# Whole chunks in each step, odd heads on the other partition half, and a fixed order to the end, in a delta-rule attention with an FFN behind it

## Chip, cores, metric

One core of a Trainium2 chip. The metric is device microseconds of a whole execution, median of the runs named. Engines: PE is TensorE, DVE VectorE, ACT ScalarE, POOL GpSimd, SP SyncE.

## The reference

```python
# attention: batch 4, heads 8, sequence 768, head_dim 48
k_n = k / (np.linalg.norm(k, axis=-1, keepdims=True) + 1e-06)
for t in range(S):
    y[:, :, t] = einsum('bhd,bhde->bhe', q[:, :, t], state)
    v_old = einsum('bhde,bhd->bhe', state, kt)
    state = state + bt * einsum('bhd,bhe->bhde', kt, vt - v_old)
# FFN: 3072 tokens, d_model 384 (= 8 heads * 48), d_ff 1536
g = x @ w_gate
out = (g / (1 + exp(-g)) * (x @ w_val)) @ w_out
```

The weights are float64 and are converted to float32 on the core; q, k, v and beta are float32. Both kernels take the sequence in 12 chunks of 64 steps. Inside a chunk the recurrence becomes matrix products: the Gram matrix K K^T is masked (call it M), the inverse Z^T of a triangular matrix made of M and beta is computed, then with the state S of the chunk before: r = V - K S, u = Z r, S += K^T u, y = Q S + (masked Q K^T) u. y of a chunk is the input x of its FFN. A 64x64 inverse is made of two 32x32 halves, done on DVE for 128 (head, half) pairs at once (`invert`), and a corner block by small matmuls (`join`).

## The kernel before: what the change touches

A unit of work is two batches of one chunk (`n`); a chunk has two units, and a group of two chunks is inverted at once.

```python
ORDER = ((0, 0), (1, 1), (0, 1), (1, 0))          # (par, b): head parity, batch
def advance(n, ps):                                # one unit
    ...                                            # K S and Q S of a unit into one p_y, r = V - K S
    yield
    for j in range(NP):
        for par, b in ORDER:
            rows = slice(64 * b, 64 * b + 64)
            nc.tensor.matmul(p_u[rows, par, j], zt[rows, u, 2*j+par], r[rows, par, j], ...)
    nc.scalar.copy(uu, p_u)
    yield
    ...                                            # S += K^T u (rows of b to rows of par)
            nc.tensor.matmul(ys[rows, par, j], pq[rows, 2*j+par], uu[rows, par, j], ...)
    nc.scalar.copy(heads(y), ys)
    yield
    ...                                            # three transposes of y, copy to x_ffn

with tc.manual_schedule(engines={PE, ACT, DVE, SP}):
    ...                                            # start, chunk 0's FFN with the weights' conversion
nc.gpsimd.memset(ztp[1], 0.0)                      # from here the compiler's scheduler orders
some(invert(1), everything)
some(joins(1, ps_one), everything)
for c in range(1, NCH):
    ...
    for bp in range(NB):
        some(advance((c + 1) * NB + bp, ps_one), everything)
    feed = ffn(c)
    for n in range(FT // 2 + NB):
        some(feed, 3 if n < FT // 2 else 1)
        some(behind, 2)                            # preparation of a later group
```

A matmul reads its two operands from the partitions of one half and writes the half in which its output lies. In p_u and in the second part of p_y, rows `b` go to rows `b`: two of the four 64x64 tiles of the array.

## Time and profile before

| | us |
|---|---|
| median of 3 runs | 907.58 (907.29 to 911.88) |
| the profiled run: metric, span | 904.54, 902.7 |
| FFN of chunk 1 starts at | 190.1 |
| from there to the last matmul | 708.4, of it PE idle 32.9 (7.9 for kn, 6.2 for the state, 6.0 for r, 9.3 around the joins and masks, 2.1 for h_f) |
| changes between 128x128 and smaller tiles in that stretch | 216 (counted record by record; the prediction has 217) |

A row of a timeline gives start, length, engine, line, operation, output<-inputs, shape and count, and in brackets the idle time before it and what ended it. The rows overlap at their ends, since ends of pipelined matmuls are modelled; differences of starts are the safe reading. In the trace each fp32 matmul of the program is two records (32 matmuls of `p_s` are "x64" for a whole chunk), transposes are one. The prediction below shows the lines.

### The profile page before, as it was taken

How to read it: one execution, taken by the hardware profiler on the slowest of the kernel's cores; microseconds unless marked ns; L12 is line 12 of the kernel's file. 1: busy time of each engine (PE TensorE's matmuls, PEld its weight loads, DVE VectorE, ACT ScalarE, POOL GpSimd, SP SyncE). 2: the span in 40 equal slices, each digit the busy share in tenths (PEclk: the TensorE clock that was granted, in tenths of full speed). 3: DMA queues.
4: the chain of work that ended last, by engine and by line, in shares of the span. 5: the costliest groups of instructions: out<-in, count | busy, mean ns of one | idle time of the engine just before them, and what ended most of it. 6: DMA issues, size and time to landing. Idle time of an engine off the chain costs nothing.

```text
span 902.7 us, 19256 instructions
## 1 busy us (share of the span) xinstructions
PE 784.2 (87%) x8648; PEld 604.9 (67%) x8648; DVE 435.9 (48%) x883; ACT 153.0 (17%) x284; POOL 87.3 (10%) x100
## 2 busy tenths in 40 slices
PE   1407787698978999998999998999998999999998
PEld 1307575376757857867857867867867768778684
DVE  4799877997238912218912219913219812001010
ACT  1104323201212112111112111112111112011010
POOL 4000112100140002210002210003110000000000
PEclk9857889798999999999999999999999999999999
DMA  6324543410031000211010211010001000000000
GB/s 167 81 39 125 146 133 102 118 27 1 12 70 37 1 20 19 45 34 31 0 22 18 45 37 27 1 28 11 10 19 20 0 20 2 1 19 1 18 1 18
DMA packets 85171, 34.38 MB, mean 38 GB/s; under 512 B 78176, under 2 KB 81248, under 8 KB 85088
## 3 DMA queue, kind: packets, MB, share of 16 engines
q1 hardware_dynamic: 78240, 27.93, 13.2%
q10 hardware_dynamic: 6848, 5.21, 2.7%
q8 instruction: 68, 1.11, 0.5%
q14 instruction: 15, 0.12, 0.0%
HBM read 28.41 MB, written 4.72 MB: 37 GB/s over the span
## 4 chain that ended last, share of the span: by engine, by line
PE 57%; DVE 32%; issue 3%; POOL 3%; ACT 2%; ACTq 2%; DMA 1%; DVEq 0%
PE p_o L560 18%; PE p_gate L540 13%; PE p_val L540 12%; DVE zb L392 7%; DVE tmp L386 6%; DVE mb L357 3%; PE p_g L313 3%; POOL norm L284 2%; DVE zt L357 2%; PE p_u L476 2%; PE p_t L302 2%; DVE h_f L553 2%; PE p_j L428 1%; PE p_y L510 1%; DVE mb L355 1%
## 5 line engine op out<-in xcount | busy, mean ns | idle before, releaser
L540 PE MATMUL p_gate<-x_ffn,wg_sb 128*128 128x256 f32 x864 | 216.8, 394 | 9.5 <-DVE wg_sb L223 8.7
L540 PE MATMUL p_val<-x_ffn,wv_sb 128*128 128x256 f32 x864 | 208.9, 386 | 0.0
L560 PE MATMUL p_o<-wo_sb,h_f 128*128 128x384 f32 x576 | 199.9, 500 | 9.4 <-DVE wo_sb L223 7.3
L540 PEld LDWEIGHTS p_gate<-x_ffn,wg_sb 128*128 128x128 f32 x864 | 162.4, 194 | 34.1 <-DVE wg_sb L223 9.5
L540 PEld LDWEIGHTS p_val<-x_ffn,wv_sb 128*128 128x128 f32 x864 | 161.8, 191 | 23.1 <-issue 0.7
L560 PEld LDWEIGHTS p_o<-wo_sb,h_f 128*128 128x128 f32 x576 | 108.8, 194 | 84.0 <-DVE wo_sb L223 11.0
L553 DVE TENSOR_TENSOR h_f<-sil,p_val 128x512 f32<-128x512 f32 x72 | 49.2, 683 | 136.0 <-PE p_val L540 135.8
L549 ACT ACTIVATE sil<-p_gate 128x512 f32<-128x512 f32 x72 | 43.0, 597 | 221.8 <-PE p_gate L540 219.5
L386 DVE TENSOR_TENSOR tmp<-zb,mb 128x31 f32<-128x31 f32 (+15 forms) x186 | 63.6, 342 | 6.0
L392 DVE TENSOR_TENSOR zb<-zb,tmp 128x31 f32<-128x31 f32 (+15 forms) x186 | 63.6, 342 | 5.7
L326 DVE TENSOR_TENSOR a_sb<-p_g,mask_k 128x512 f32<-128x512 f32 x24 | 16.5, 688 | 85.8 <-PE p_g L313 85.8
L284 POOL TENSOR_TENSOR norm<-norm,half 128x8 f32<-128x8 f32 x24 | 39.5, 1648 | 139.0 <-DVE norm L281 134.2
L302 PE MATMUL p_t<-ident,kn 128*128 128x128 f32 x96 | 23.5, 304 | 29.5 <-DVE kn L288 19.1
L422 DVE COPY t<-p_j 32x256 f32<-32x256 f32 x20 | 8.4, 422 | 80.8 <-ACT t L421 80.8
L568 ACT COPY o_sb<-p_o 128x384 f32<-128x384 f32 x24 | 11.5, 478 | 181.4 <-PE p_o L560 181.4
L417 PE MATMUL p_j<-zt,a_sb 32*32 32x32 f32 x768 | 17.4, 198 | 25.8 <-DVE zt L355 25.8
L417 PEld LDWEIGHTS p_j<-zt,a_sb 32*32 32x32 f32 x768 | 14.9, 113 | 34.7 <-issue 29.2
L302 PEld LDWEIGHTS p_t<-ident,kn 128*128 128x128 f32 x96 | 14.1, 153 | 33.8 <-issue 13.7
L303 ACT COPY kq<-p_t 128x1024 f32<-128x1024 f32 (+1 forms) x28 | 24.6, 889 | 69.1 <-PE p_t L302 69.1
L313 PE MATMUL p_g<-kq 64*64 64x128 f32 (+1 forms) x896 | 29.5, 280 | 7.6 <-ACT kq L303 4.5
L313 PEld LDWEIGHTS p_g<-kq 64*64 64x64 f32 x896 | 23.9, 151 | 16.9 <-ACT kq L303 11.1
L457 PE MATMUL p_y<-state,kq 64*64 64x48 f32 x1408 | 28.4, 221 | 6.2 <-DVE state L502 6.2
(79 smaller groups left out, 633.8 us busy)
## 6 DMA issues: line engine op xcount, KB each, us to landing
wo_sb<-in_moe_w_gate_dram SPq DMA_DIRECT2D x9, 512.0 KB
wo_sb<-in_moe_w_val_dram SPq DMA_DIRECT2D x9, 512.0 KB
qpad<-in_q_dram SPq DMA_DIRECT2D x48, 96.0 KB
vin<-in_v_dram SPq DMA_DIRECT2D x48, 96.0 KB
out_dram<-o_sb ACTq DMA_DIRECT2D x48, 96.0 KB
kin<-in_k_dram SPq DMA_DIRECT2D x44, 96.0 KB
staged<-in_moe_w_out_dram SPq DMA_DIRECT2D x6, 384.0 KB
zt<-in_moe_w_out_dram SPq DMA_DIRECT2D x6, 384.0 KB
```

Of the source, the lines that this page charges most:

```text
L284: nc.gpsimd.tensor_tensor(out=norm, in0=norm, in1=half, op=ALU.pow)
L302: nc.tensor.transpose(p_t[:, j, at], (kn, qn)[x][:, pair], ident)
L313: nc.tensor.matmul(p_g[cols, par, j, xs[0] : xs[-1] + 1], kq[n][rows, j, 0, cols], kq[n][rows, j, xs[0] : xs[-1] + 1, cols],)
L357: nc.vector.transpose(out(rows, 0), in_(rows, 0))
L386: nc.vector.tensor_tensor(out=t_v, in0=zb[:, 0 : j + 1, j : j + 1].to_broadcast([128, j + 1, m]), in1=mb[:, j : j + 1, j + 1 : R].to_broad ...
L392: nc.vector.tensor_tensor(out=zb[:, 0 : j + 1, j + 1 : R], in0=zb[:, 0 : j + 1, j + 1 : R], in1=t_v, op=ALU.add,)
L417: nc.tensor.matmul(p_j[64 * b : 64 * b + R, h], a[lo, h, 0:R], zt[lo, u, h, R:C])
L457: nc.tensor.matmul(dst[cols, par, j], kqn[rows, j, x, cols], st[rows, b, j], start=(x == 0 and j == 0), stop=(x == 0), skip_group_check=True,)
L540: nc.tensor.matmul(ps[name][:, i], w_sb[:, t, (f + i) * 128 : (f + i + 1) * 128], x[:, t], start=(t == 0), stop=(t == KT - 1),)
L549: nc.scalar.activation(sil, ps[name], ACTF.Silu)
L553: nc.vector.tensor_tensor(out=hs[-1][:, f % 4 : f % 4 + 2], in0=sil, in1=ps["p_val"], op=ALU.mult)
L560: nc.tensor.matmul(p_o, hs[f // 4][:, f % 4, bp * 128 : (bp + 1) * 128], wo_sb[:, f], start=(f == 0), stop=(f == FT - 1),)
```

## The change

Three things at once: whole chunks in each step; M, Z and V of the odd heads on the other partition half, so that all four array tiles work; a fixed order of all engines to the end.

```diff
-    def advance(n, ps):
+    def advance(c):                       # both units of a chunk
-                rows = slice(64 * b, 64 * b + 64)
-                nc.tensor.matmul(p_u[rows, par, j], zt[rows, u, 2*j+par], r[rows, par, j], ...
+        for bp, j, par, b, first in every():
+            nc.tensor.matmul(
+                p_u[half_of(b), par, bp, j],
+                zt[half_of(b ^ par), par, bp, j],
+                r[half_of(b ^ par), par, bp, j], ...
...                                        # likewise p_r, p_y, gram of K, vin, beta
-    beta_b = const.tile(...)              # 16 transfers issued by ACT
+    nc.scalar.dma_start(out=beta_n, in_=beta.rearrange("b h s -> (b h) s"))
...                                        # and 48 tiny matmuls that turn it
+    def point(c):                         # before each of 6 FFN steps and 2 output blocks
+        n = c + 1
+        mine = n < NCH and steps("advance", n) < 4 and may_advance(n)
+        if mine and steps("advance", n) > 0:
+            step("advance", advance, n)
+        elif prep_step(c):
+            if c == 0:
+                prep_step(c)
+        elif mine:
+            step("advance", advance, n)
+        norm_step()
...                                        # fill(c, k): k small steps of invert on DVE
-    with tc.manual_schedule(engines=engines):
-        ...                               # chunk 0 only
-    for c in range(1, NCH): ...
+    with tc.manual_schedule(engines={PE, Activation, DVE, SP, Pool}):
+        ...
+        for c in range(NCH):
+            ffn(c, point, fill)
```

The join, too, is laid over twice as many 32x32 tiles, and the number of PSUM buffers of the FFN goes from three to four.

## The prediction

> **What bounds the kernel now.** I read first the page's busy shares and slices, then TensorE's (PE's) timeline by stretch, then the DVE timeline of the first 215 us, last the table of stretches. The page:
>
> ```profile
> span 902.7 us, 19256 instructions
> ...
> PE   1407787698978999998999998999998999999998
> PEld 1307575376757857867857867867867768778684
> DVE  4799877997238912218912219913219812001010
> ...
> PEclk9857889798999999999999999999999999999999
> ```
>
> A slice is 22.6 us. For eight slices DVE is nearly full and PE has holes and a low clock; afterwards PE is nearly full and DVE mostly idle. The table of stretches gives the same in numbers, split at 190.1 us:
>
> ```profile
> 0.00:190.10 190.10, 108.65 (x1484) 83.72 (x1485) 153.44 (x309) 43.98 (x79) 29.76 (x42) 0.81 0.43 109
> 190.10:898.50 708.40, 675.53 (x7165) 521.14 (x7163) 282.50 (x575) 108.57 (x204) 57.57 (x58) 0.99 0.09 19
> ```
>
> (Columns: us, then busy PE, PEld, DVE, ACT, POOL; clock, DMA share, GB/s.) The split is where the second of twelve chunks' FFN begins. PE's timeline around it, and at three later places:
>
> ```profile
> 174.89 2.93 PE L560 MATMUL p_o<-wo_sb,h_f 128*128 128x384 f32 x4 [0.96 <-DVE wo_sb L223]
> 178.82 11.46 PE L560 MATMUL p_o<-wo_sb,h_f 128*128 128x384 f32 x28 [1.00 <-DVE wo_sb L223]
> 190.12 2.75 PE L540 MATMUL p_gate<-x_ffn,wg_sb 128*128 128x256 f32 x12
> ...
> 547.64 1.13 PE L540 MATMUL p_val<-x_ffn,wv_sb 128*128 128x256 f32 x4
> 548.70 0.68 PE L492 MATMUL p_s<-uu,kn 64*64 64x48 f32 x32
> 549.20 1.10 PE L510 MATMUL p_y<-uu,p_sb 64*64 64x48 f32 x32
> 550.23 0.70 PE L540 MATMUL p_val<-x_ffn,wv_sb 128*128 128x256 f32 x2
> ...
> 592.88 0.69 PE L417 MATMUL p_j<-zt,a_sb 32*32 32x32 f32 x32
> ...
> 880.26 2.75 PE L540 MATMUL p_val<-x_ffn,wv_sb 128*128 128x256 f32 x12
> 882.85 15.64 PE L560 MATMUL p_o<-wo_sb,h_f 128*128 128x384 f32 x48
> ```
>
> The difference of starts is the cost: 12 gate or val records take 2.59 us, 48 p_o records 15.5. So a chunk's FFN is 12 x 2.59 + 15.5 = 46.6 us, and no part of the change touches it. p_s (32 records, 0.50 us) and p_y (32 records, 1.03 us) have the same shape: p_s goes over four combinations of input and output halves, p_y over two.
>
> **Budget of 190 to 898 us in the kernel before.** FFN: 11 x 46.6 = 512. Attention, from such differences: per chunk, state products 2 x 1.03, p_u 2 x 1.06, p_s 2 x 0.50, p_y 2 x 1.03, p_f 6 x 0.109 = 7.9, ten times 79; products of a chunk 16 transposes x 0.109 + 2 x 1.03 = 3.8, eight times 30; joins 40 x 0.63 = 25. Idle: 708.4 - 675.5 = 33. Along the timeline I count 217 changes between 128x128 matmuls and smaller tiles; one round trip lengthens the run (4 p_val records from 547.64 take 1.06 instead of 0.86), so some 0.1 us a change: 22. Sum 701 of 708; 7 stay unexplained.
>
> **What the Trainium skill says.** "TensorEngine Tiling (Array Packing)", Key Properties: different tiles work in parallel, and changing the tiling mode drains the array. The trace agrees: 0.50 against 1.03 us, and 0.1 us a change. The same page, Gotcha 1: different row tiles can't use one PSUM bank at once. The trace can't tell here: in p_u of before two row tiles do share a bank, but so few tiles work that it shows nothing. "TensorE: Matmul & The Clock Gate", Part 1 on the floor of small matmuls, says start-to-start never drops below about 25 ns; the trace has 64 state records in 1.03 us, 16 ns, so the floor does not bind here. "GPSIMD Engine Reference", the table's row on SBUF interfaces, says they are shared with VectorE; the trace agrees: one tiny DVE add took 2.51 us beside a GpSimd memset at 12 us, 0.16 elsewhere.
>
> **The change, part by part.**
>
> (a) Four tiles. p_u and p_y fall from 33 to 16 ns a record: 2 x 1.05 us a chunk. The joins, now over twice as many 32x32 tiles, fall from 20 ns to between 10 and 16: I take 12.5, 1280 records, 16 us against 25. Gram is cut into K and Q halves, twice as many records at half the columns: 2.2 us instead of 2.06. So attention in the second stretch: (2.06 + 1.03 + 1.0 + 1.03 + 0.65) = 5.8 x 10 = 58; (1.74 + 2.2) x 8 = 31; 16. Sum 105 against 134.
>
> (b) Fewer changes of mode. I followed the new schedule by hand through the points (eight a chunk: one before each of six FFN steps and two output blocks). A chunk has three small-tile blocks of `advance`, one of gram, half of two joins: 48 blocks in the second stretch, 96 changes, 10 us against 22.
>
> (c) Waits. The four steps of `advance(c+1)` now stand at four successive points of FFN c, with 5 us of FFN matmuls between them; the longest thing between two steps is three ACT copies (3 x 0.48). So r, uu, y and x_ffn are ready when PE comes. By the same walk this fails once: chunk 2 needs the inverse of group 1, which ends in the last block of FFN 1, so the second join and four steps of `advance(2)` stand bare: copies of 1.0, 0.95, 0.85, 1.4 and 0.85 us plus hand-overs, some 6.5 us. Idle 6.5 against 33.
>
> Second stretch after: 512 + 105 + 10 + 6.5 + the unexplained 7 = 641, against 708.
>
> (d) Head. The kernel before issues 16 beta transfers from ACT (15 of them take 12.49 us), so the first copy of kq waits until 19.8 us. One transfer and 48 tiny matmuls replace them. K alone is prepared before the inversion, and no conversion stands ahead of it. K of chunk 0 lands at about 5.5 us; two chunks' square, sum, power, scaling (0.95 each on DVE at 128x768, power up to 3 us on GpSimd), transposes, cold gram (1.96 per 64 records) and two masks of 1.25 bring the inversion to start at 21 instead of 34.7. It lasts 36.5 as before, plus six small transposes (2.6) and the Q mask (1.25): 62. Then six conversions at 2.7 with a copy and the state between: 79.5, where before stood 88.6.
>
> (e) Weights. 24 conversions remain: 12 x 2.7 + 4 x 2.2 + 8 x 1.95 = 57 us of DVE. Before, they ended at 179.2, since DVE also had 16 us of other work, 4.5 of stretching beside GpSimd and 13 of waits. After: masks of chunks 2 and 3 come behind the last conversion, so 10 of other work, 4, and 5 of waits: end at 79.5 + 76 = 155.5. Then the last of p_o, the products of chunk 3 (6 us with a copy that PE must await) and the second block of 7.75: FFN 1 starts at 170, against 190. The inversion of group 1, on DVE from 179 to 214 before, now goes in small steps beside FFN 1.
>
> Sum: 170 + 641 + 4.2 (last row's end to span's end) = 815; the metric stands 4.9 above the span (907.58 against 902.7): 820. The estimate of waits in (e) is the softest; with half of them 817. I say **818 us**, a factor of 0.90.
>
> **Rivals.** *Fixed order brings new waits.* px and py are single buffers, four engines run strictly in order, and invert steps stand between h_f's. For it: during an inversion DVE has about 49 us of work in a chunk of 58, and the conversions show how a DVE wait passes to PE (L223 lines above). Against: h_f has four PSUM buffers, a full FFN step (5.2 us) of slack, and steps are a point apart. At 1 us for each of the 80 later points: near 895, still at best same; at a quarter, 838. *The head does not move*, being 57 us of conversions and 73 of two inversions on DVE: then only the second stretch gains, 902.7 - 67 + 4.9 = 841. Against: the second inversion leaves the head's path in the new order. *Row tiles collide in a bank* (p_u and p_y use both banks from both row halves): they keep 33 ns, 2.1 x 10 = 21 more, 839. Against: in each output half the two row tiles use different banks.
>
> **Range and chances.** The middle of the three rivals in part gives 840 to 845; everything a little better (waits 0, the joins at 10 ns, no unexplained 7, FFN 1 at 165) gives 800. So 798 to 845. 2% faster is 889.4; only the first rival at full size reaches it. Chances: faster 0.96, same 0.03, slower 0.01.
>
> **What would show it.** Right: 32 p_u records and 32 p_y records each in about 0.52 us; PE idle under 15 us after the second chunk's start, and that start near 170; the inversion starting near 21; gate-to-gate periods of 59 us a chunk in the middle; one bare gap before FFN 2. Wrong: p_u still at 33 ns (bank rival); brackets of 1 us with r, uu or kn at many points (order rival); last wo_sb conversion still near 179 (head rival). If PE's idle stays above 40 us in the second stretch, step (c) has failed.

## The result

815.92 us median of 4 runs (815.01 to 817.87), against 907.78 (907.29 to 911.88) for the kernel before in the same rounds. The ratio is 0.8991 (95% interval 0.8955 to 0.9027): the mean of one kernel's fast runs over the mean of the other's in the same rounds, so not quite the ratio of the medians. Outputs are correct in all runs.

The page of the kernel after, busy shares in 40 slices of 20.4 us:

```profile
span 816.2 us, 20536 instructions
...
PE   3304868399989999999999999999999999999997
...
DVE  3899799849824785207881157852277511011010
...
PEclk9655899599998999999999999999999999999999
```

From the ninth slice on PE is full but for the twelfth (224 to 245 us), and there are eight weak slices before, as in the kernel before. The table of stretches, cut where chunk 1's FFN starts, with the columns of the prediction's table:

```profile
182.35:811.80 629.45, 623.38 (x7741) 495.40 (x7739) 283.72 (x502) 103.57 (x164) 48.47 (x34) 0.99 0.11 21
```

So the head (all before chunk 1's FFN) gained 190.1 - 182.35 = 7.8 us in these two traces and the second stretch 79 (708.4 against 629.6 to the end of the last matmul). PE's timeline in the middle of it (the p_r and first p_y are the state products, the second p_y is that with u):

```profile
441.59 1.15 PE L484 MATMUL p_r<-state,kt 64*64 64x48 f32 x64
442.56 1.11 PE L493 MATMUL p_y<-state,qt 64*64 64x48 f32 x64
443.60 2.86 PE L574 MATMUL p_gate<-x_ffn,wg_sb 128*128 128x256 f32 x12
446.30 2.75 PE L574 MATMUL p_val<-x_ffn,wv_sb 128*128 128x256 f32 x12
448.98 1.15 PE L505 MATMUL p_u<-vin,zt 64*64 64x48 f32 x64
450.06 2.86 PE L574 MATMUL p_gate<-x_ffn,wg_sb 128*128 128x256 f32 x12
```

64 records of p_u now take 1.08 us with the change of mode behind them, where 32 took 1.06 before; and no row has a bracket. In the whole stretch the brackets sum to 6.0 us (629.45 - 623.38 = 6.1 in the table), 5.5 of them in the one bare stretch before chunk 2's FFN (the 6.6 in e4's expectation has one wait twice), and PE changes between 128x128 and smaller tiles 90 times. A join's 128 records take 1.21 us from start to start, where 32 took 0.63:

```profile
225.89 1.29 PE L446 MATMUL p_j<-zt,a_sb 32*32 32x32 f32 x128
227.10 8.01 PE L595 MATMUL p_o<-wo_sb,h_f 128*128 128x384 f32 x24
```

The head looks different from what was foreseen. PE and then ACT in the kernel after, around the end of the weights' conversion:

```profile
136.91 1.04 PE L336 MATMUL p_t<-ident,kn 128*128 128x128 f32 x8
...
156.84 1.99 PE L346 MATMUL p_g<-kt 64*64 64x64 f32 x64 [18.02 <-ACT kt L337]
...
160.46 9.17 PE L595 MATMUL p_o<-wo_sb,h_f 128*128 128x384 f32 x24
```

```profile
150.88 1.12 ACT L186 ACTIVATE power<-power,rebias 128x384 int32<-128x384 uint32 x2 [2.77 <-DVE power L178]
154.77 1.12 ACT L186 ACTIVATE power<-power,rebias 128x384 int32<-128x384 uint32 x2 [2.77 <-DVE power L178]
155.80 0.99 ACT L337 COPY kt<-p_t 128x1024 f32<-128x1024 f32 x1
```

The transposes of chunk 2's K are done at 138.0 (136.91 + 1.04), but their copy runs at 155.8: in ACT's fixed order it stands behind the activations of the last conversions, each of which waits for DVE. PE's order has the gram of chunk 2 next, so PE stands 18 us, and the output block p_o, of which most could have run, begins only at 160.5.

### The profile page after: what moved, and what is told of

Read it like the earlier page. It is cut to its first block, busy times and chain, and to the rows that moved or that the text cites. A ratio compares the mean times of both kernels' runs of the same rounds, so it can differ in the third digit from the quotient of the medians.

```text
span 816.2 us, 20536 instructions
## 1 busy us (share of the span) xinstructions
PE 719.5 (88%) x9384; PEld 573.6 (70%) x9384; DVE 430.8 (53%) x768; ACT 145.0 (18%) x230; POOL 80.5 (10%) x73
## 4 chain that ended last, share of the span: by engine, by line
PE 77%; DVE 15%; issue 4%; DMA 2%; POOL 1%; ACT 1%; ACTq 0%; POOLq 0%; DVEq 0%
PE p_gate L574 22%; PE p_o L595 21%; PE p_val L574 21%; PE p_g L346 2%; PE p_t L336 2%; DVE mant L199 2%; DVE power L208 2%; DVE zb L410 1%; DVE tmp L404 1%; PE p_u L505 1%; PE p_y L535 1%; DVE mant L190 1%; PE p_s L522 1%; PE p_r L484 1%; PE p_y L493 1%
## 5 line engine op out<-in xcount | busy, mean ns | idle before, releaser
L574 PE MATMUL p_gate<-x_ffn,wg_sb 128*128 128x256 f32 x864 | 205.7, 388 | 0.0
L574 PE MATMUL p_val<-x_ffn,wv_sb 128*128 128x256 f32 x864 | 198.7, 379 | 0.5 <-DVE wv_sb L217 0.5
L314 POOL TENSOR_TENSOR norm<-norm,half 128x16 f32<-128x16 f32 x12 | 35.4, 2953 | 165.4 <-DVE norm L308 163.6
L318 POOL TENSOR_TENSOR kn<-kin,norm 128x768 f32<-128x768 f32 x10 | 14.8, 1479 | 293.6 <-DVE norm L317 246.6
L359 DVE TENSOR_TENSOR a_sb<-p_g,mask_k 128x1024 f32<-128x1024 f32 x12 | 14.7, 1223 | 45.2 <-PE p_g L346 45.2
L346 PE MATMUL p_g<-kt 64*64 64x64 f32 x768 | 16.1, 244 | 19.1 <-ACT kt L337 19.1
L346 PEld LDWEIGHTS p_g<-kt 64*64 64x64 f32 x768 | 14.5, 156 | 23.2 <-ACT kt L337 19.6
L186 ACT ACTIVATE power<-power,rebias 128x512 int32<-128x512 uint32 (+1 forms) x30 | 19.9, 677 | 58.4 <-DVE power L178 56.2
L372 DVE STREAM_TRANSPOSE zt<-zb 32x1024 f32<-32x1024 f32 x12 | 26.3, 2188 | 0.1
L372 DVE STREAM_TRANSPOSE mb<-a_sb 32x1024 f32<-32x1024 f32 x12 | 25.6, 2136 | 0.3
```

The costliest lines, as they stand in the source:

```text
L186: nc.scalar.activation(power.bitcast(I32), power, ACTF.Relu, bias=rebias, scale=8.0)
L314: nc.gpsimd.tensor_tensor(out=norm, in0=norm, in1=half, op=ALU.pow)
L346: nc.tensor.matmul(p_g[half_of(b if of_q else b ^ par), par, bp, j], kt[c][half_of(par), bp, j, b], xt[half_of(par), bp, j, b],)
L372: nc.vector.transpose(out(rows, 0), in_(rows, 0))
L574: nc.tensor.matmul(ps[name][:, i], w_sb[:, t, (f + i) * 128 : (f + i + 1) * 128], x[:, t], start=(t == 0), stop=(t == KT - 1),)
```

## Experiments

My theory after the result: four things make the second stretch shorter, namely tiles, fewer changes of mode, steps placed at points, and (perhaps) the fixed order; and in the head one wait made by the fixed order gives back a part. In each run the kernel before ran in the same rounds on the same chip.

| run | us, median | ratio to before | 95% interval |
|---|---|---|---|
| the change | 815.92 | 0.8991 | 0.8955 to 0.9027 |
| e1 two tiles | 835.55 | 0.9203 | 0.9171 to 0.9234 |
| e2 p_o first | 809.48 | 0.8912 | 0.8878 to 0.8946 |
| e3 bare steps | 859.17 | 0.9460 | 0.9430 to 0.9491 |
| e4 free order | 853.76 | 0.9398 | 0.9362 to 0.9434 |
| e5 cut blocks | 827.94 | 0.9123 | 0.9095 to 0.9150 |
| e6 more beta | 817.84 | 0.9006 | 0.8978 to 0.9034 |
| e7 bare and free | 856.82 | 0.9431 | 0.9388 to 0.9474 |
| e8 the change again | 816.94 | 0.9002 | 0.8977 to 0.9027 |
| e9 p_o first again | 808.49 | 0.8905 | 0.8881 to 0.8930 |

### e1: the odd heads back on the same half

```diff
-                    s = 64 * (b ^ par)
+                    s = 64 * b
-                zt[half_of(b ^ par), par, bp, j],
-                r[half_of(b ^ par), par, bp, j],
+                zt[half_of(b), par, bp, j],
+                r[half_of(b), par, bp, j],
...            # the same in gram of K, p_r, p_y, beta_t and the copies of y
```

> The changed kernel with the odd heads' M, Z and V put back on the same partition half as the even heads', all else equal (same order on every engine). My theory: p_u and the second p_y go back to two of four array tiles and to 33 ns a record, 2 x 1.05 us more for each of the ten chunks that PE bounds, so about 837 us against 816; 64 records of p_u take 2.1 us instead of 1.05. Rival, that the tiles do not matter because PE waits elsewhere: 816 to 819.

Measured 835.55, 19.6 more than the change. All engines run the same instructions in the same order. PE's timeline of e1:

```profile
387.71 2.07 PE L505 MATMUL p_u<-vin,zt 64*64 64x48 f32 x64
389.71 2.86 PE L574 MATMUL p_gate<-x_ffn,wg_sb 128*128 128x256 f32 x12
```

2.00 us from start to start against 1.08. The theory holds: in these two blocks the four tiles are worth about 20 us; PE hardly waits there (5.1 us idle in the stretch in e1, 6.1 in the change), so the time shows as it is summed.

### e2: the output block of chunk 0 ahead of the waiting gram

```diff
-            if c == 0:
+            if c == 0 and first:
                 prep_step(c)
...
             ffn(c, point, fill)
+            if c == 0:
+                prep_step(0)
...
-                    fill(c, 2)
+                    fill(c, 3 if c == 1 else 2)
```

> In chunk 0's FFN the preparation of chunk 2 and 3 is spread, one step before each output block and one after, instead of two before each; the invert steps in FFN 1 go from five to six a step to make up for it. Theory: the 18 us for which PE stood before the gram products of chunk 2 came from ACT's fixed order (the copy of kt stands behind the last eight conversions' activations), and kept p_o from running beside those conversions; with p_o ahead of the gram, FFN 1 starts near 171 instead of 182 us, and the whole takes 804 to 809. Rival, that p_o would have waited for the last converted weights on DVE all the same: 814 to 818, with the wait of 18 us now in front of p_o.

Measured 809.48. PE's timeline of e2:

```profile
137.53 2.10 PE L595 MATMUL p_o<-wo_sb,h_f 128*128 128x384 f32 x6
140.66 0.91 PE L595 MATMUL p_o<-wo_sb,h_f 128*128 128x384 f32 x2 [1.03 <-DVE wo_sb L217]
...
155.75 2.93 PE L595 MATMUL p_o<-wo_sb,h_f 128*128 128x384 f32 x4 [0.96 <-DVE wo_sb L217]
158.61 1.71 PE L346 MATMUL p_g<-kt 64*64 64x64 f32 x64
```

The wait of 18 us is gone; p_o runs beside the conversions, waiting for each in turn, and ends with them at 158.6. Chunk 1's FFN starts at 174.0 instead of 182.35 (expected near 171). That ACT's order made PE wait is read from ACT's timeline above. e2 leaves that order (the copy of kt runs at 153.6, behind the conversions there too) and takes PE out of its way, so it shows what the wait cost: 8.4 us between these two traces, 6.4 in the medians, half a microsecond outside the range expected (804 to 809). The second stretch hardly differs: 630.8 us in e2's trace, 629.6 in the change's. Single traces differ by some 3 us here: in the seven with this head (the change, e1, e3, e4, e5, e7, e8) chunk 1's FFN starts between 179.8 and 182.4.

### e3: the steps placed bare behind the FFN

```diff
-        mine = n < NCH and steps("advance", n) < 4 and may_advance(n)
+        mine = n < 3 and steps("advance", n) < 4 and may_advance(n)
```

> From chunk 3 on the four steps of advance stand one after the other behind the FFN of the chunk before, and no longer at its points; the rest is the same. Theory: each of nine chunks then shows a bare stretch like the one before FFN 2 (14 us for 5.8 us of matmuls), 8 us each, less 0.4 for fewer changes of mode: about 884 us (870 to 895). Rival, that the gain came from tiles and fewer changes of mode and not from hiding the steps: at most 825.

Measured 859.17: 43 us more, not 68. PE's timeline of e3, one bare stretch:

```profile
421.81 1.15 PE L484 MATMUL p_r<-state,kt 64*64 64x48 f32 x64
422.78 1.11 PE L493 MATMUL p_y<-state,qt 64*64 64x48 f32 x64
424.75 1.15 PE L505 MATMUL p_u<-vin,zt 64*64 64x48 f32 x64 [0.86 <-DVE vin L501]
426.81 1.15 PE L522 MATMUL p_s<-uu,kn 64*64 64x48 f32 x64 [0.92 <-ACT uu L514]
...
430.52 0.88 PE L556 MATMUL p_f<-ident,y 128*128 128x128 f32 x6 [1.62 <-ACT y L546]
```

It lasts 431.23 - 421.81 = 9.4 us for 5.8 of matmuls. I had taken the size from the one bare stretch of the change, in front of chunk 2's FFN, 14 us; there the granted clock had fallen (64 records of p_y took 2.30 us of modelled length instead of 1.11), which happens in only some of e3's. The brackets after chunk 1's start sum to 35.8 us in e3, 30 more than in the change, 16 of them for y and 9 for uu. The rest of the 43 goes with a clock of 0.95 to 0.98 in most of e3's stretches of 100 us, where the change has 1.00 from 300 us on; and this although PE changes its mode 54 times instead of 90. The placing does matter; its size per chunk was overestimated.

### e4: the order of chunks 1 to 11 left to the compiler

```diff
-        for c in range(NCH):
-            ffn(c, point, fill)
-            ...
+        chunk(0)
+    for c in range(1, NCH):            # outside the fixed order
+        chunk(c)
```

> The fixed order ends after chunk 0, so that the compiler's own scheduler orders everything from chunk 1 on, as in the kernel before; the program's text is the same. Theory: the placing of the steps at the points does the work, and the fixed order as such little: 808 to 826. Rival, that the fixed order to the end is what removed the waits: the idle of PE after chunk 1's start rises from 6.6 to some 30 us as before, 838 or more.

Measured 853.76, 38 more than the change. My theory fell and the rival's figure came: with the same program text the compiler's scheduler brings the idle to 33.8 us, 27.6 of it in seven waits for h_f. These are not the waits of before, where h_f stood for 2.1 of 32.9: with the steps at the points the waits between steps stay away in e4 too (from chunk 3 on 1.1 us, for vin), and a new kind takes their place. One wait in PE's timeline of e4, with the p_val whose buffer it needs, then DVE's before it:

```profile
411.42 2.75 PE L574 MATMUL p_val<-x_ffn,wv_sb 128*128 128x256 f32 x12
...
429.15 5.49 PE L574 MATMUL p_val<-x_ffn,wv_sb 128*128 128x256 f32 x12 [4.75 <-DVE h_f L587]
```

```profile
421.85 0.33 DVE L404 TENSOR_TENSOR tmp<-zb,mb 128x175 f32<-128x175 f32 x1
425.01 0.17 DVE L316 TENSOR_SCALAR norm<-norm 128x16 f32<-128x16 f32 x1 [2.82 <-POOL norm L314]
...
428.41 0.68 DVE L587 TENSOR_TENSOR h_f<-sil,p_val 128x512 f32<-128x512 f32 x1
```

The h_f at 428.4 is that of the p_val from 411.42, which ended at 414.2: it runs 14.2 us late, after 4.0, 6.6 and 9.7 us for the three before it, behind inversion steps and an add for which DVE stood 2.8 us waiting for GpSimd's power. In the change h_f follows its p_val by 0.1 us in most cases. The FFN has four PSUM buffers, and the p_val at 429.15 needs the one that this h_f frees. PE stands, its granted clock is 0.5 from 427.9 to 434.7, and the next 12 records of p_val take 5.4 us from start to start instead of 2.6. So four buffers alone do not keep the waits away.

### e5: every block of small tiles cut in two

```diff
+            if c > 2:
+                yield "half"           # between p_r and p_y; in p_u; between p_s and p_y; between the grams
...
+                    rest()             # the second half, between gate and val or inside p_o
```

> From chunk 3 on each block of small-tile matmuls (state products, p_u, p_s with p_y, the two grams) is cut in two, with half of an FFN step or of an output block between; the matmuls are the same and so are all other instructions. Some 34 blocks more, 68 changes of mode. Theory: a change costs 0.1 us, so 7 us more: 821 to 825 against 816. Rival, that a change of mode costs nothing of note and the 0.1 us read in the timeline is only the end of the pipeline: 815 to 818.

Measured 827.94, 12.0 more than the change by the ratios. The matmuls are the same. PE's timeline of e5, the step that was shown for the kernel after:

```profile
444.64 1.15 PE L484 MATMUL p_r<-state,kt 64*64 64x48 f32 x64
445.72 2.86 PE L580 MATMUL p_gate<-x_ffn,wg_sb 128*128 128x256 f32 x12
448.51 1.15 PE L495 MATMUL p_y<-state,qt 64*64 64x48 f32 x64
449.59 2.86 PE L580 MATMUL p_val<-x_ffn,wv_sb 128*128 128x256 f32 x12
452.38 0.68 PE L509 MATMUL p_u<-vin,zt 64*64 64x48 f32 x32
```

From p_r to p_u it takes 452.38 - 444.64 = 7.74 us, in the kernel after 448.98 - 441.59 = 7.39: 0.35 for two changes more. In all there are 146 changes instead of 90 (I had expected 68 more, it is 56). The second stretch is 641.4 us instead of 629.6, 1.7 of the difference idle; 10.1 / 56 = 0.18 us a change. So a change of mode costs about 0.18 us here, nearly twice what I had read, and the theory holds with that size.

### e6: beta by 16 transfers again

```diff
-    nc.scalar.dma_start(out=beta_n, in_=beta.rearrange("b h s -> (b h) s"))
+    for i in range(16):
+        part = slice(i * S // 16, (i + 1) * S // 16)
+        nc.scalar.dma_start(out=beta_n[:, part], in_=beta.rearrange("b h s -> (b h) s")[:, part])
```

> beta comes by 16 transfers issued by ACT instead of by one, all else equal. Theory: in the kernel before ACT's 16 issues at 0.7 us held back the first copies; here they let the last part of beta land near 17 us instead of 10, PE's 48 small matmuls stand behind that and the transposes of K behind those, so the inversion starts 5 to 7 us later (near 30 instead of 24.3) and, DVE being the bound up to 158 us, the whole takes 821 to 823. Rival, that the earlier start came from moving the conversion and the Q work behind the inversion: 815 to 818.

Measured 817.84, within the intervals of the change. DVE's timeline of e6, the masks and the first step of the inversion:

```profile
22.50 2.36 DVE L363 TENSOR_TENSOR a_sb<-p_g,mask_k 128x1024 f32<-128x1024 f32 x2 [4.31 <-PE p_g L350]
24.89 2.15 DVE L373 STREAM_TRANSPOSE mb<-a_sb 128x1024 f32<-128x1024 f32 x1
```

The inversion starts at 24.9 instead of 24.3 (22.8 to 24.3 in the traces with the change's head). ACT issues until 15.4 us in e6 (4.5 in the change) and runs its first copy at 17.0 (11.9), but K of both chunks is scaled only at 16.1, and the transposes and grams follow at once. My theory fell: in this order the issues cost about 2 us at most. What else moved the start from 34.7 to 24.3 (K of both chunks before anything that waits for PE; the conversion and the Q work behind) was not taken apart.

### e7: bare steps and free order together

```diff
# e4, and in it
-        mine = n < NCH and ...
+        mine = n < 3 and ...
```

> Both at once: the steps of advance written one after the other behind each FFN from chunk 3 on, and the order left to the compiler's scheduler from chunk 1 on; so the form that the kernel before had, with four tiles and whole chunks. Fixed order with bare steps took 859, placed steps with free order 854, both 816. Theory: the scheduler fills the bare stretches by itself but puts work before what PE needs, so this lands at 845 to 875, near each of the two, and the gain needs both. Rival, that the losses add: 890 to 900.

Measured 856.82: as e3 and e4, not their sum. Idle after chunk 1's start is 31.5 us, 9.4 of it for uu, 4.0 for vin and 3.8 for h_f. Together with e3 and e4 this is a square: bare and free 857, bare and fixed 859, placed and free 854, placed and fixed 816. Either half of the idea alone brings next to nothing (3 us at most); the two together bring 41 us. The three slow corners are alike in time and not in cause: the bare ones wait between the steps, e4 waits for h_f. Why the scheduler puts so much of the inversion ahead of h_f in e4 was not looked into.

### e8 and e9: the change and e2 side by side

> The changed kernel once more, unchanged, on one chip with the next one, so that the two can be compared within the same rounds: 814 to 819.

> The kernel of e2_po_first once more, unchanged. If the 6 us between it and the changed kernel are real, 807 to 811 here with the changed kernel at 814 to 819, and intervals apart; if they were chance, within 2 us of each other.

816.94 and 808.49; the intervals of the ratios, 0.8977 to 0.9027 and 0.8881 to 0.8930, are apart. The version of e2 is the fastest, 1.0% ahead of the change. In these two traces chunk 1's FFN starts at 180.5 and 175.0.

One more idea, the first step of the conversion on GpSimd instead of DVE, did not compile in the form tried and was not run.

## Why the prediction was right, and where its steps were not

The time said was 818, the time measured 815.9. That it came so close is luck: two errors of about 12 us cancelled, the head being 12 longer than said and the second stretch 11 shorter. The mechanism of the second stretch was right in its terms; of the prediction's own signs p_u and p_y at 0.52 us for 32 records (0.52 to 0.54), idle under 15 us, periods of 59 us in the middle (57.5 to 60.5) and the one bare gap came true, FFN 1 near 170 and the inversion near 21 did not.

- **Tiles (a): right.** p_u and p_y came to 16 to 17 ns a record; e1 puts their worth at 20 us (21 in the sum). The join was better than taken: 128 records in 1.21 us, 9.5 ns instead of 12.5, so 12 us for all instead of 16.
- **Changes of mode (b): the count right (90 against 96), the price only one end of it.** 0.1 us was read off the FFN records around one round trip, and there it holds: against 2.59 and 15.5 us for undisturbed groups, the FFN's records at full clock are 21.8 us longer before (216 changes) and 8.6 after (90), 0.10 a change both times. e5 gives 0.18 for the whole; the other part lies within the small blocks, and the prediction had it in the costs that it took from differences of starts. So the sum did not suffer. The "unexplained 7" is none of this price: 4.0 of it are FFN records of before at half clock, 3.0 are attention blocks that took 137 us instead of the 134 in the budget. I carried the 7 into the sum for after unchanged, where FFN and attention came to 623.5, against 627 in the sum.
- **Waits (c): right in size, 6.1 us idle against 6.5, and right in place** (the one gap before chunk 2's FFN). The reason was only half there. The sum credits the placing at points alone; e4 shows that the same placing in a free order idles 33.8 us. The rival that I weighed ran the wrong way: I had the fixed order as a source of waits, while after chunk 1's start it is what keeps the waits for h_f away.
- **Second stretch in all: 629.6 against 641.** 4 us by the join, 7 by the remainder that should not have been carried over.
- **Head (d): 24.3 against 21 for the inversion, 83.7 against 79.5 for the sixth conversion.** PE's cold transposes (1.97 us for eight) and grams (3.69 for 128 records) and K of chunk 1 landing only at 10.1 are the slower parts. The part given to ACT's 16 issues is not borne out: e6 has about 2 us for it at most in the new order.
- **Weights (e): the last conversion ended at 158.4 against 155.5; the step from there to chunk 1's FFN failed.** The prediction has p_o running beside the conversions and FFN 1 at 170. It stood behind the gram, the gram behind a copy, the copy in ACT's order behind the last conversions: FFN 1 at 182.35. This is the "order" rival after all, in one place, with 18 us of wait; the version that avoids it is 6.4 us (e2) and 8.4 us (e9 against e8) faster.
- **From span to metric.** I added 4.9 us, the median less the profiled span. But the profiled run of before was one of its fastest (904.54), and within one run the two differ by 1.8. The difference of the spans is 86.5 us, that of the medians 91.9; the runs of before go from 904.5 to 913.5, and why was not looked into.

Where the 79 us of the second stretch went, then, from the two traces by differences of starts with the brackets left out: p_u and the second p_y 19 (41.5 to 22.7), the joins 13 (25.3 to 12.2), idle 27 (32.9 to 6.1), the FFN's own records 17 (538.5 to 521.3, the matmuls being the same: 13 with 126 fewer changes of mode, 4 by the clock), all else 3. Of these e1 varies the first, e3, e4 and e7 the third and e5 the fourth; the joins' part is read from the traces alone.

## What to carry to other kernels

In this kernel, steps with a chain of small dependencies made PE wait for almost nothing (6 us in 630) once each stood one long piece of independent matmul work behind the one before and the order that was written was the order that ran: e3, e4 and e7 lie within 5.4 us of one another, and the two together gain 41. A fixed order needs a look at every engine's own list: an engine that drains PSUM must not have a queue of work that waits for a slower engine ahead of the copy that PE needs next. And before summing waits, count changes of the array's mode; at e5's price 126 changes fewer are 22 us, about as much as the tiles of p_u and p_y.

## What the Trainium skill lacked or had wrong

- "TensorEngine Tiling (Array Packing)", Key Properties, says that changing the tiling mode drains the array but gives no cost. Here it is about 0.18 us a change (e5: 56 changes, 10.1 us).
- The same page, Gotcha 1, says that different row tiles cannot use one PSUM bank at once, and does not limit this to one set of output partitions. In the kernel after, p_y of the state products has one bank per row tile, while p_y with u has both row tiles in each bank, apart by output half: 64 records take 1.04 us from start to start in both (442.56 to 443.60 and 456.41 to 457.45), with correct outputs. So in different output halves a shared bank cost nothing here; within one half no run tests it. It is this page's wording that is too wide.
- "TensorE: Matmul & The Clock Gate", Part 1, has a floor of about 25 ns from start to start. The 128 records of a join take 1.21 us; as two records are one fp32 matmul, that is 9.5 ns a record and 19 a matmul, on four different 32x32 tiles. The prediction compared records with the floor; per matmul p_r, with 64 records in 0.97 us, is at 30 ns and does not contradict it, the join does. The page treats matmuls packed on different tiles in a part of its own, so it is only the "never" of Part 1 that the join contradicts.
- No page that I found gives the cost of a power on GpSimd: 1.65 us for 128x8 elements (before), 2.9 to 3.0 for 128x16 (after).
